# Mixer with seven-tap attention in fp32: h's own ready times in the planner, the u_parts chain cut in two, a fifth tap tile, a fourth val tile

## The chip, the cores and the metric

The kernel runs on one core of one Trainium2 chip. The metric is the time of one execution in microseconds. Before the change three runs took 2129.74, 2135.10 and 2135.57 us, median 2135.1 us.

## The reference

An array x of 8 x 4096 x 192 goes through a seven-tap weighted sum with softmax weights, and the result through an MLP over the tokens and an MLP over the channels:

```python
w = np.exp(weight_gen - max); w = w / (w.sum(-1) + 1e-9)        # 7 taps, 8 heads
x = einsum('bshk,bskhg->bshg', w, windows of 7 rows of x)       # 8 x 4096 x 192
h  = np.maximum(x.transpose(0, 2, 1) @ w_tok1, 0) @ w_tok2      # 4096 -> 256 -> 4096
u  = x + h.transpose(0, 2, 1)
h2 = np.maximum(u @ w_ch1, 0) @ w_ch2                           # 192 -> 1536 -> 192
out = u + h2
```

The weights of the MLPs come as 64-bit floats. Products that must be exact to fp32 are made from a high part and a low part of each operand.

## The kernel before

The 32768 rows are cut into 64 chunks of 512 rows (`NG`), eight to a batch. A prologue makes the tap sums and the first token product of the first batch. Then follow 64 **stages**, one for each chunk g, and the text calls the stage of chunk g "stage g". A stage has the following work.

- **Channel 1** (`channel1`, line 565): six pairs p of PSUM tiles `ph`, 18 matmuls each, from `u_hi` and `u_lo` of chunk g and the resident weights.
- **take_h** (line 577): ScalarE makes the high part of the ReLU (line 579), VectorE the low part (line 580). The tile `h` has four buffers and `ps_w`, from which `ph`, `up` and `th` come, has three. So the fourth `ph` of a stage cannot start until the first `h` has been read by VectorE.
- **Channel 2** (`channel2`, line 584): six times ten matmuls into `acc`; three of them show as x30. The fifth and sixth `h` are taken after its first and second.
- **Token 2** of chunk g+1 (`token2`, line 512; tile `up`): ScalarE copies `xb` into PSUM (line 518), ten matmuls (line 524), ScalarE and VectorE then make `uf` (lines 531 to 536), and `u_parts` (line 538) makes `u_hi` and `u_lo` from it, eight ScalarE copies and two VectorE subtractions, for channel 1 of the next stage. It is one chain: the three copies of lines 550 to 552 stand behind the subtractions of lines 548 and 549.
- **Token 1** of a chunk some eight stages ahead (`token1`, line 475; tile `th`). For the first two batches it is an fp32 product (line 507), after that a product of parts (lines 490 and 492). Its sum over the batch is carried in `h1s`. The last of a batch is followed by `make_h1`, on which token 2 of the next batch rests.
- **Attention** (`attention`, line 204) of two chunks at a time: softmax on `wg`, fourteen products (line 211) and six additions (line 225) on VectorE; the first product goes to `xa`, the other taps to `pr` tiles (four buffers), and GpSimd adds each pair sum to `xa` by DMA (line 229).
- **Store** (`store`, line 638): two transposes on VectorE, twelve ScalarE copies into `out_tile` (line 655), two DMAs.
- **Conversions** in the first stages only: `convert` (line 146) turns 64-bit weights into fp32, three ScalarE and three VectorE operations in a `val` tile, and `split` makes high and low parts. `w2s` is converted in three parts, the last of them in stage 0 (`convert_channel("c2", 2)`, lines 453 to 455).

What runs in which order is set by a planner that runs while the program is built. It keeps estimated clocks `at` of the engines; work waits in chains; `pump` issues from the chains whatever fits before the next matmul group, ScalarE by priority and VectorE by earliest start. The result is one fixed instruction list for each engine, which each engine follows in order.

## Time and profile before

| what | value |
|---|---|
| profiled execution | 2131.6 us |
| its span, first to last instruction | 2129.8 us |
| three runs | 2129.74, 2135.10, 2135.57 us |
| TensorE busy | 2085.4 us, 98% of the span |
| VectorE busy | 1538.5 us, 72% |
| ScalarE busy | 1440.3 us, 68% |
| mean granted TensorE clock | 0.996 |

The times of stages are read from the rows of the TensorE timeline: a stage runs from the first `ph` matmul of its channel 1 to that of the next stage. In a row the number in brackets is the idle time ahead of its first instruction and what ended it.

### The profile page before, as it was taken

Reading aid. Unit: us, or ns where it says so; the run is one execution under the profiler, and the core shown is the slowest. Engines: PE = TensorE matmul, PEld = TensorE weight load, DVE = VectorE, ACT = ScalarE, POOL = GpSimd, SP = SyncE. Lnnn points to the kernel's source line nnn. Section 1 sums busy time; section 2 is a strip of 40 time slices with the busy share of each in tenths; the row PEclk is TensorE's granted clock in tenths of the full one; section 3 lists DMA queues with packets and bytes.
Section 4 is the critical chain, followed back from the end, with each engine's and each line's share of the span. In section 5 each row is a group of like instructions: output and inputs, shape, how many; then the busy total and the mean of one; then the engine's idle time right before and its main releaser. Section 6 shows DMA issues by size and latency. Waiting matters only on the chain.

```text
span 2129.8 us, 32140 instructions
## 1 busy us (share of the span) xinstructions
PE 2085.4 (98%) x12766; PEld 1691.5 (79%) x12766; DVE 1538.5 (72%) x1760; ACT 1440.3 (68%) x2226; POOL 158.2 (7%) x194
## 2 busy tenths in 40 slices
PE   7989899999999999999999999999999999999998
PEld 5767788787878888888888888888888888888887
DVE  8978988788887777777777877777787765343433
ACT  5568666667766766676676677667666766766665
POOL 0001111000100010000000010000100000000000
PEclk9999999999999999999999999999999999999999
DMA  8666757878687667566766756676665655321221
GB/s 279 225 213 171 207 147 210 253 200 230 185 234 202 189 172 190 150 182 181 196 189 173 200 156 174 171 202 193 173 194 149 181 163 148 89 66 45 64 63 23
DMA packets 166198, 363.82 MB, mean 171 GB/s; under 512 B 16552, under 2 KB 105896, under 8 KB 150688
## 3 DMA queue, kind: packets, MB, share of 16 engines
q1 hardware_dynamic: 139808, 285.74, 42.8%
q0 software_dynamic: 25344, 74.46, 17.8%
q8 instruction: 100, 1.64, 0.3%
q10 hardware_dynamic: 896, 1.57, 0.2%
q14 instruction: 50, 0.41, 0.1%
HBM read 225.13 MB, written 70.52 MB: 139 GB/s over the span
## 4 chain that ended last, share of the span: by engine, by line
PE 82%; DVE 10%; ACT 4%; DMA 3%; issue 2%; POOL 0%; SPq 0%; ACTq 0%; DVEq 0%; POOLq 0%
PE acc L591 36%; PE ph L573 33%; PE up L524 7%; PE th L490 3%; DVE h L580 2%; DVE pr L211 2%; PE th L492 1%; DVE prk L327 1%; DMA raw<-in_moe_w_tok_dram 1%; PE th L507 1%; DMA xt<-in_x_dram 1%; DMA xa<-pr 1%; DVE val L160 1%; DVE val L159 1%; DVE pr L225 1%
## 5 line engine op out<-in xcount | busy, mean ns | idle before, releaser
L591 PE MATMUL acc<-h,w2s 128*128 128x512 f32 x3800 | 884.5, 390 | 2.5 <-DVE w2s L454 2.5
L591 PEld LDWEIGHTS acc<-h,w2s 128*128 128x128 f32 x3800 | 709.2, 188 | 148.9 <-DVE w2s L454 2.9
L579 ACT ACTIVATE h<-ph 128x1024 fp32r<-128x1024 f32 x384 | 394.4, 1027 | 396.2 <-PE ph L573 340.1
L580 DVE SCALAR_TENSOR_TENSOR h<-ph,h 128x1024 fp32r<-128x1024 f32 x384 | 467.1, 1217 | 121.3 <-ACT h L579 120.8
L573 PE MATMUL ph<-u_hi,w_hi 64*128 64x512 f32 x2304 | 343.5, 396 | 13.8 <-ACT u_hi L550 5.8
L573 PE MATMUL ph<-u_hi,w_lo 64*128 64x512 f32 x2304 | 332.9, 389 | 0.0
L573 PE MATMUL ph<-u_lo,w_hi 64*128 64x512 f32 x2304 | 332.4, 388 | 0.0
L211 DVE TENSOR_TENSOR pr<-xt,wg 128x768 f32<-128x768 f32 x336 | 314.0, 949 | 8.9 <-DMA xa<-pr 8.1
L573 PEld LDWEIGHTS ph<-u_hi,w_hi 64*128 64x128 f32 x2304 | 216.8, 185 | 82.8 <-issue 21.5
L573 PEld LDWEIGHTS ph<-u_hi,w_lo 64*128 64x128 f32 x2304 | 221.9, 185 | 47.3
L573 PEld LDWEIGHTS ph<-u_lo,w_hi 64*128 64x128 f32 x2304 | 221.8, 185 | 47.4 <-ACT u_lo L554 0.6
L229 POOL DMA_DIRECT2D xa<-pr x168 | 144.6, 861 | 1439.0 <-DVE pr L225 1236.9
L536 DVE TENSOR_TENSOR uf<-up,uf 64x512 f32<-64x512 f32 x63 | 43.0, 682 | 243.2 <-ACT uf L532 243.2
L655 ACT COPY out_tile<-oa 32x256 f32<-32x256 f32 x504 | 203.5, 404 | 7.8
L524 PE MATMUL up<-w,h 128*128 128x512 f32 x630 | 161.7, 402 | 5.9 <-ACT up L518 5.9
L225 DVE TENSOR_TENSOR pr<-pr 128x768 f32<-128x768 f32 x168 | 160.3, 954 | 3.7
L524 PEld LDWEIGHTS up<-w,h 128*128 128x128 f32 x630 | 113.8, 188 | 48.8 <-ACT up L518 16.2
L518 ACT COPY up<-xb 128x1024 f32<-128x1024 f32 x63 | 64.0, 1016 | 84.6 <-DVE h L580 81.5
L490 PE MATMUL th<-xh,w 128*128 128x384 f32 x384 | 112.5, 358 | 1.1 <-ACT th L483 1.1
L655 ACT COPY out_tile<-oc 32x256 f32<-32x256 f32 x252 | 101.6, 403 | 11.0 <-DVE oc L648 6.8
L269 DVE TENSOR_TENSOR xh<-xa,xh 128x768 fp32r<-128x768 f32 x48 | 45.9, 955 | 73.3 <-ACT xh L266 73.3
L492 PE MATMUL th<-xh,w 128*128 128x192 f32 x384 | 96.2, 250 | 0.0
(86 smaller groups left out, 1717.8 us busy)
## 6 DMA issues: line engine op xcount, KB each, us to landing
w<-s SPq DMA_DIRECT2D x96, 1024.0 KB, 5.3
xa<-pr POOLq DMA_DIRECT2D x168, 384.0 KB, 4.9
xt<-in_x_dram SPq DMA_DIRECT2D x56, 960.0 KB, 9.8
out_dram<-out_tile SPq DMA_DIRECT2D x128, 192.0 KB, 3.2
xs<-t SPq DMA_DIRECT2D x58, 384.0 KB, 4.6
xb<-xs SPq DMA_DIRECT2D x348, 64.0 KB, 5.0
raw<-in_moe_w_tok_dram SPq DMA_DIRECT2D x16, 1024.0 KB, 6.0
s<-w POOLq DMA_DIRECT2D x8, 1024.0 KB, 5.3
```

The lines of the kernel that those rows point to most:

```text
L211: nc.vector.tensor_mul(t.rearrange("p t (h g) -> p (t h) g", h=H).rearrange("p (o n) g -> p o n g", o=1), x_k, w)
L225: nc.vector.tensor_add(sums[m], sums[m], prt.pop(m))
L229: nc.gpsimd.dma_start(xat[m].rearrange("p t d -> p (t d)"), sums[m].rearrange("p t d -> p (t d)"), accum_op=ALU.add)
L490: nc.tensor.matmul(th[:, r, 0:2 * D], w[:, c, 0, rs], xh[:, c, :], start=i + c == 0, stop=False, skip_group_check=True)
L492: nc.tensor.matmul(th[:, r, 0:D], w[:, c, 1, rs], xh[:, c, 0:D], start=False, stop=c == CT - 1, skip_group_check=True)
L518: nc.scalar.copy(up.rearrange("p k (n b c) -> p (k n) c b", c=CT, b=Q), xb.rearrange("p k (n c b) -> p (k n) c b", c=CT, b=Q))
L524: nc.tensor.matmul(up[:, n, :], h1[:, k, d], w[:, l, k * N:(k + 1) * N], start=k == 0 and j == 0 and not seeded, stop=k == KR - 1 and j == ...
L573: nc.tensor.matmul(ph[:, j, :], w[rows, k, p * P:(p + 1) * P], u[rows, k], start=n == 0, stop=n == len(steps) - 1)
L579: nc.scalar.activation(h[:, :, 0, :], ph, AF.Relu)
L580: nc.vector.scalar_tensor_tensor(h[:, :, 1, :], ph, 0.0, h[:, :, 0, :].bitcast(F32), op0=ALU.max, op1=ALU.subtract)
L591: nc.tensor.matmul(acc[:, n, :], w2s[:, f, d], h[:, j, l, :], start=False, stop=f == NF - 1 and i == len(steps) - 1, skip_group_check=True)
L655: nc.scalar.copy(dst, src[to:to + Q].rearrange("p (n e d) -> p n e d", n=2, d=Q)[:, n])
```

## The change

- `u_parts` becomes two chains. The first holds `u_hi[:, 0]`, `u_hi[c, 2]`, the subtractions and the three `u_lo` copies, the second the three other `u_hi` copies.
- `PR` goes from 4 to 5.
- `val` gets four buffers outside the prologue pool and two inside (before three and three); `ident` moves into the prologue's pool. The planner waits for a free `val`, and weights of token 1 are fetched two chunks ahead instead of one.
- The planner keeps a ready time for each `h` (`h_at[p]`) and not one for the last. `SLACK_M` is 1000 (400), `LATER` 4000 (5000). An fp32 token 1 no longer waits for the token 1 of the chunk ahead of it.
- A token 1 that is not ready at the usual places may run ahead of the last group of channel 2. The wait for the last part of `w2s` stands ahead of the group that reads it, one group later than before.

```diff
-    PR = 4
+    PR = 5
...
-        pool = pro if pro is not None and n % 6 >= 3 else p1
-        return pool.tile([P, NV], F32, tag="val", name="val", bufs=3)
+        pool = pro if pro is not None and n % 6 >= 4 else p1
+        return pool.tile([P, NV], F32, tag="val", name="val", bufs=2 if pool is pro else 4)
...
+        yield "w", 0, lambda: free["val"]
         v = val_tile()[:, 0:n]
...
-        yield "gate", 0, lambda: state["token1"] >= m - 1
+        if m // NCH >= F1:
+            yield "gate", 0, lambda: state["token1"] >= m - 1
...
+        def first():
+            yield from begin()
+            yield "u", 620, lambda: act(hi[:, 0], ua)
+            yield "u", 620, lambda: act(hi[c, 2], uc[c])
+            yield "n", 0, lambda: taken.update(at=at["act"] + HOP)
+            yield "v", 610, lambda: dve(lo[:, 0], ua, hi[:, 0].bitcast(F32))
+            yield "v", 610, lambda: dve(lo[c, 2], uc[c], hi[c, 2].bitcast(F32))
+            yield "u", 620, lambda: act(lo[c, 1], f[e, 0])
+            yield "u", 620, lambda: act(lo[e, 1], f[c, 0])
+            yield "u", 620, lambda: act(lo[e, 2], f[c, 2])
+            yield "n", 0, last
+
+        def second():
+            yield from begin()
+            yield "gate", 0, lambda: "at" in taken
+            yield "u", 620, lambda: act(hi[c, 1], ua[e])
+            yield "u", 620, lambda: act(hi[e, 1], ua[c])
+            yield "u", 620, lambda: act(hi[e, 2], uc[c])
+            yield "n", 0, last
+        return first(), second()
...
-    LATER = 5000
+    LATER = 4000
...
-    SLACK_M = 400
+    SLACK_M = 1000
...
-        while state["w1"] < min(m + 1 + (m >= F1 * NCH - 3), NG - 1):
+        while state["w1"] < min(m + 2, NG - 1):
...
-        chains.insert(3, Chain(u_parts(m), t, ("u", m)))
+        chains[3:3] = [Chain(items, t, ("u", m)) for items in u_parts(m)]
...
-                if p == 0:
-                    h_at = w_at[-1]
+                h_at[p] = w_at[-1]
...
-                if g == 0:
-                    need(lambda: ("c2", 2) in done, (convert_channel, "c2", 2))
...
+            if g == 0 and p == 2 * NP // 3:
+                need(lambda: ("c2", 2) in done, (convert_channel, "c2", 2))
+            if p == NP - 1:
+                run_picked(picked)
             channel2(g, p)
-            on("pe", C2, free["acc"] if p == 0 else 0.0, h_at)
+            on("pe", C2, free["acc"] if p == 0 else 0.0, h_at[p])
...
+            if p == NP // 2 and token1_ready(C2) and ready[0][0] <= g + NCH:
+                picked = [(do_token1, begin_token1())]
```

The lists of the engines differ in nearly every stage. TensorE's differs in stages 2 to 7 alone, and there in where the eight fp32 token 1 products stand. Three places follow.

**End of stage 0, ScalarE.** Rows `val` of 768 elements belong to the last part of `w2s`, `up` is the copy ahead of token 2 of chunk 1, `h` the sixth of the stage. Before:

```order
L166 CAST w_867<-val 128x1024
L155 ACTIVATE val<-raw 128x768
L156 ACTIVATE val<-val,below 128x768
L518 COPY up<-xb_79 128x8x4x32
L579 ACTIVATE h<-ph 128x2x512
L157 ACTIVATE val<-val 128x768
L155 ACTIVATE val<-raw 128x1024
L181 ACTIVATE wg<-wg 128x448
L531 COPY uf<-up 64x512
L532 COPY uf<-up 128x512
L453 CAST w2s<-val 128x4x192
```

Now:

```order
L165 CAST w_869<-val 128x1024
L520 COPY up<-xb_74 128x8x4x32
L597 ACTIVATE h<-ph 128x2x512
L154 ACTIVATE val<-raw 128x768
L155 ACTIVATE val<-val,below 128x768
L180 ACTIVATE wg<-wg 128x448
L533 COPY uf<-up 64x512
L534 COPY uf<-up 128x512
L156 ACTIVATE val<-val 128x768
L454 CAST w2s<-val 128x4x192
L561 CAST u_hi<-uf 128x512
L562 CAST u_hi<-uf 64x512
```

The two first steps of the conversion now stand behind `up` and the sixth `h`, and its third behind the copies of `uf`.

**Start of stage 3, VectorE.** Rows `oa` and `oc` are the store of stage 2; the last row is the first `h` of stage 3. Before:

```order
L159 SCALAR_TENSOR_TENSOR val<-raw,val 128x1024
L211 TENSOR_TENSOR xa<-xt,wg 128x768
L160 SCALAR_TENSOR_TENSOR val<-raw,val 128x1024
L211 TENSOR_TENSOR xa<-xt,wg 128x768
L645 STREAM_TRANSPOSE oa<-acc 128x512
L646 STREAM_TRANSPOSE oc<-acc 128x512
L648 TENSOR_TENSOR oc<-oc 64x512
L161 SCALAR_TENSOR_TENSOR val<-raw,val 128x1024
L211 TENSOR_TENSOR pr<-xt,wg 128x768
L580 SCALAR_TENSOR_TENSOR h<-ph,h 128x2x512
```

Now:

```order
L291 STREAM_TRANSPOSE t<-xa 128x768
L181 TENSOR_REDUCE mx<-wg 128x64
L158 SCALAR_TENSOR_TENSOR val<-raw,val 128x1024
L663 STREAM_TRANSPOSE oa<-acc 128x512
L664 STREAM_TRANSPOSE oc<-acc 128x512
L666 TENSOR_TENSOR oc<-oc 64x512
L159 SCALAR_TENSOR_TENSOR val<-raw,val 128x1024
L598 SCALAR_TENSOR_TENSOR h<-ph,h 128x2x512
```

The two products into `xa` and the product into `pr` have gone behind the four `h` of the stage.

**Stages 7 and 8, TensorE and ScalarE.** TensorE from the end of channel 1 of stage 7 on; `th` is token 1, `acc` channel 2, `up` token 2 of chunk 8. Before:

```order
L507 MATMUL th<-xa,val 128x192 x8
L591 MATMUL acc<-h,w2s 128x512 x30
L507 MATMUL th<-xa,val 128x192 x8
L591 MATMUL acc<-h,w2s 128x512 x30
L507 MATMUL th<-xa,val 128x192 x8
L524 MATMUL up<-w_2708,h_3145 128x512 x10
```

Now:

```order
L509 MATMUL th<-xa,val 128x192 x8
L609 MATMUL acc<-h,w2s 128x512 x30
L509 MATMUL th<-xa,val 128x192 x8
L609 MATMUL acc<-h,w2s 128x512 x30
L526 MATMUL up<-w_2694,h_3090 128x512 x10
```

The last token 1 of the batch now has a half of channel 2 between itself and token 2. ScalarE in stage 8, from the last `u_hi` of chunk 8 to the first `h`. Before:

```order
L552 CAST u_hi<-uf 64x512
L553 CAST u_lo<-u_lo 64x512
L554 CAST u_lo<-u_lo 64x512
L555 CAST u_lo<-u_lo 64x512
L655 COPY out_tile<-oa 32x8x32 x4
L166 CAST w_3151<-val 128x4x256
L579 ACTIVATE h<-ph 128x2x512 x3
```

Now:

```order
L576 CAST u_hi<-uf 64x512
L566 CAST u_lo<-u_lo 64x512
L567 CAST u_lo<-u_lo 64x512
L568 CAST u_lo<-u_lo 64x512
L673 COPY out_tile<-oc 32x8x32 x2
L673 COPY out_tile<-oa 32x8x32 x4
L673 COPY out_tile<-oc 32x8x32 x2
L673 COPY out_tile<-oa 32x8x32 x4
L165 CAST w_3096<-val 128x4x256
L597 ACTIVATE h<-ph 128x2x512 x3
```

All twelve copies of the store of stage 7 now stand between `u_lo` and the first `h`; before, eight of them came earlier.

More of the change, by code (lines that the diff above doesn't have):

```diff
@@ L56, in mixer_kernel @@
     pro = None
-    ident = const.tile([P, P], F32, name="ident")
-    make_identity(nc, ident)
     below = const.tile([P, 1], F32, name="below")
@@ L411, in last @@
             state["vals"] -= 1
+            free["val"] = at["dve"] + HOP
             w2t[i] = t
@@ L458, in last @@
             state["vals"] -= 1
+            free["val"] = at["dve"] + HOP
             done.add((which, n))
@@ L543, in u_parts, with begin @@
         f, act, dve = lo.bitcast(F32), nc.scalar.copy, nc.vector.tensor_sub
-        yield "gate", 0, lambda: state["channel1"] >= m
-        yield "w", 0, lambda: free["parts"]
-        yield "u", 620, lambda: act(hi[:, 0], ua)
-        yield "u", 620, lambda: act(hi[c, 2], uc[c])
-        yield "v", 610, lambda: dve(lo[:, 0], ua, hi[:, 0].bitcast(F32))
-        yield "v", 610, lambda: dve(lo[c, 2], uc[c], hi[c, 2].bitcast(F32))
-        yield "u", 620, lambda: act(hi[c, 1], ua[e])
-        yield "u", 620, lambda: act(hi[e, 1], ua[c])
-        yield "u", 620, lambda: act(hi[e, 2], uc[c])
-        yield "u", 620, lambda: act(lo[c, 1], f[e, 0])
-        yield "u", 620, lambda: act(lo[e, 1], f[c, 0])
-        yield "u", 620, lambda: act(lo[e, 2], f[c, 2])
-        def last():
-            ut[m] = hi, lo
-            free["u"] = at["act"] + HOP
-        yield "n", 0, last
+        left = [0, 1]
+        taken = {}
+        def begin():
+            yield "gate", 0, lambda: state["channel1"] >= m
+            yield "w", 0, lambda: free["parts"]
+        def last():
+            left.pop()
+            if not left:
+                ut[m] = hi, lo
+                free["u"] = at["act"] + HOP
+        def first():
[17 more added lines that the diff above has]
+        return first(), second()
     ht, acc_t = {}, {}
@@ L696, in mixer_kernel @@
     w_at, h1_at, h1s_at = deque([0.0] * 3), {0: 0.0}, [0.0]
-    free = {"acc": 0.0, "u": 0.0, "t": 0.0, "parts": 0.0, "xh": 0.0}
+    free = {"acc": 0.0, "u": 0.0, "val": 0.0, "t": 0.0, "parts": 0.0, "xh": 0.0}
     pr_free = deque([0.0] * PR)
@@ L794, in mixer_kernel @@
              "summed": NCH - 1, "turned": FT - 1, "parts": NCH - 1, "kept": FT - 1, "stored": -1, "out": -1,
-             "done": NCH - 1, "w1": NCH, "channel1": 0, "rest": 0}
+             "done": NCH - 1, "w1": NCH + 1, "channel1": 0, "rest": 0}
     def raw_free(tag):
@@ L851, in mixer_kernel @@
             tc.tile_pool(name="ps_pro", bufs=1, space=bass.MemoryType.PSUM) as ps_pro:
+        ident = pro.tile([P, P], F32, name="ident")
+        make_identity(nc, ident)
         warm = pro.tile([P, 1], F32, name="warm")
@@ L863, in start @@
             items = iter(items)
-            for _ in range(4):
+            for _ in range(5):
                 next(items)[2]()
@@ L939, in mixer_kernel @@
             nc.tensor.matmul(w[:, j, :], w1_hi[:, 0, 0:P], w1_hi[:, 0, 0:512], start=True, stop=True)
-    run(u_parts(0))
+    run(*u_parts(0))
     free["u"] = 0.0
@@ L947, in mixer_kernel @@
     add_chain(load_w1(NCH))
+    add_chain(load_w1(NCH + 1))
     state["token2"] = 0
@@ L1012, in mixer_kernel @@
     for g in range(NG):
-        phs, kept = {}, {}
+        phs, kept, h_at = {}, {}, {}
         soon = ((convert_w2, 1),) if g == 0 else ()
@@ L1062, in mixer_kernel @@
                 take_h(g, p + HB, phs[p + HB])
-                h_at = on("dve", LOW, on("act", TOP, at["pe"]))
+                h_at[p + HB] = on("dve", LOW, on("act", TOP, at["pe"]))
                 if kept[p] in w_at:
-                    w_at[w_at.index(kept[p])] = h_at
+                    w_at[w_at.index(kept[p])] = h_at[p + HB]
                 if last:
                     picked += list(it)
-                    h_at = 0.0
+            if p == NP // 2 and token1_ready(C2) and ready[0][0] <= g + NCH:
+                picked = [(do_token1, begin_token1())]
         pump(at["pe"] + SLACK_M)
```

## The prediction

> **What bounds the kernel now.** I read the page's busy times and slices first, then the chain that ended last, in order of time, then TensorE's waits, and last the timelines of the three engines around each wait.

> ```profile
> span 2129.8 us, 32140 instructions
> PE 2085.4 (98%) x12766; PEld 1691.5 (79%) x12766; DVE 1538.5 (72%) x1760; ACT 1440.3 (68%) x2226; POOL 158.2 (7%) x194
> PE   7989899999999999999999999999999999999998
> DVE  8978988788887777777777877777787765343433
> PE 82%; DVE 10%; ACT 4%; DMA 3%; issue 2%; POOL 0%; SPq 0%; ACTq 0%; DVEq 0%; POOLq 0%
> ```

> TensorE is the bound, and what it idles it idles in the first slices, where VectorE is nearly as full as TensorE. How long a stage is without waits comes from the chain:

> ```profile
> 319.76 2.60 PE th L507 x16
> ...
> 1000.65 12.49 PE ph L573 x108
> ...
> 1031.54 12.49 PE ph L573 x108
> ...
> 1924.78 12.49 PE ph L573 x108
> ...
> 1953.38 12.49 PE ph L573 x108
> ```

> Channel 1 takes 12.49 us, a stage without token 1 28.60 (1924.78 to 1953.38), with the later token 1 30.89 (1000.65 to 1031.54); an fp32 token 1 adds 2.60, so 31.20. Now the starts of the stages, and the waits that speak for themselves:

> ```profile
> 123.45 0.50 PE L573 MATMUL ph<-u_hi,w_hi 64*128 64x512 f32 x2
> ...
> 154.47 4.85 PE L591 MATMUL acc<-h,w2s 128*128 128x512 f32 x20 [2.46 <-DVE w2s L454]
> ...
> 192.20 0.50 PE L573 MATMUL ph<-u_hi,w_hi 64*128 64x512 f32 x2
> 194.69 1.66 PE L573 MATMUL ph<-u_hi,w_hi 64*128 64x512 f32 x4 [1.99 <-ACT u_hi L550]
> ...
> 227.28 0.97 PE L573 MATMUL ph<-u_hi,w_hi 64*128 64x512 f32 x6
> ...
> 236.84 0.97 PE L573 MATMUL ph<-u_hi,w_hi 64*128 64x512 f32 x6 [3.12 <-DVE h L580]
> ...
> 255.06 4.55 PE L507 MATMUL th<-xa,val 128*128 128x192 f32 x16 [1.81 <-ACT th L483]
> ...
> 266.36 0.97 PE L573 MATMUL ph<-u_hi,w_hi 64*128 64x512 f32 x6
> ```

> ```profile
> 396.88 2.56 PE L524 MATMUL up<-w,h 128*128 128x512 f32 x10 [2.35 <-ACT up L518]
> 401.41 0.49 PE L573 MATMUL ph<-u_hi,w_hi 64*128 64x512 f32 x2 [1.97 <-ACT u_hi L546]
> 402.77 1.95 PE L573 MATMUL ph<-u_hi,w_hi 64*128 64x512 f32 x4 [0.86 <-ACT u_hi L550]
> ...
> 418.34 2.58 PE L524 MATMUL up<-w,h 128*128 128x512 f32 x10
> ...
> 436.74 0.97 PE L573 MATMUL ph<-u_hi,w_hi 64*128 64x512 f32 x6
> ...
> 629.98 0.97 PE L573 MATMUL ph<-u_hi,w_hi 64*128 64x512 f32 x6
> ```

> These rows give the excess over stages without waits, waits and slow matmuls together. Stages 0 and 1: 192.20 - 123.45 - 57.20 = 11.55 us. Stage 2: 35.08 - 31.20 = 3.88. Stage 3: 39.08 - 31.20 = 7.88. Stages 4 to 8 (six fp32 token 1, one later one): 170.38 - 160.89 = 9.49. Stages 9 to 14: 193.24 - 6 x 30.89 = 7.90. In all **40.7 us**; this is the most that any order of the same matmuls can gain behind the prologue. From 629.98 on stages run at their length.

> ```profile
> PE ph L573 <- ACT u_hi L550: 5.8, 4, 2.0
> PE ph L573 <- DVE h L580: 5.5, 4, 3.1
> ```

> Two lines of TensorE's waits: `u_hi` is late four times and `h` four times. The change works on both.

> **The change part by part.** The prologue keeps its list on TensorE, and `ident` is needed first at 11.8 us; I cost its move at nothing, hidden behind the first tap products. No matmul is added or removed.

> *Stages 0 to 2.* The last part of `w2s` comes later:

> ```profile
> 147.98 0.84 ACT L157 ACTIVATE val<-val 128x768 f32<-128x768 f32 x1
> ...
> 153.12 0.83 ACT L453 CAST w2s<-val 128x768 fp32r<-128x768 f32 x1 [1.61 <-DVE val L161]
> ```

> The third step stood at 147.98, now it stands behind both copies of `uf`, which end near 151.3 whatever stands ahead. It ends at 152.2, three VectorE steps of 0.95 end at 155.1, the cast at 155.9, the first subtraction (0.42) at 156.4. TensorE then waits until 156.4 and not 154.47: **2.0 us lost**. In return all `u_hi` are ready at 159, ahead of channel 1. But four `val` steps of 1.1 us now stand ahead of the `u_lo` copies, which end near 165.2, and channel 1 of stage 1 uses them 1.6 us after its start: the first group ends some 1.4 us later than before. Stage 1 comes out 0 to 2 us later. In stage 2 the 1.99 us for `u_hi` and some 1.7 us of slow matmuls behind it go. What is late next is `h`: VectorE is full from the sixth `h` of stage 1 to the first of stage 2 (nine steps, the store, two products and an addition ahead of it, some 14 us), and I work out 1.7 us for the fourth `ph`. Together I take -0.5, with bounds of -5 (the `u_hi` waits of stages 1 and 2, 3.4, and 1.7 of slow matmuls go, nothing comes) and +4 (2.0 for `w2s`, 2 for stage 1).

> [...] The trace does not follow the gap's length: after 3.12 us at 236.84 six matmuls take 0.97 as without a wait, while after 1.81 us at 255.06 sixteen take 4.55. [...]

> *Stage 3.* Ahead of its first `h` VectorE had two `xa` products, a `val` step and a `pr` product:

> ```profile
> 233.56 1.22 DVE L161 SCALAR_TENSOR_TENSOR val<-raw,val 128x1024 uint32<-128x1024 uint32 x1
> 234.71 0.95 DVE L211 TENSOR_TENSOR pr<-xt,wg 128x768 f32<-128x768 f32 x1
> 235.57 1.22 DVE L580 SCALAR_TENSOR_TENSOR h<-ph,h 128x1024 fp32r<-128x1024 f32 x1
> ...
> 253.49 1.14 ACT L155 ACTIVATE val<-raw 128x1024 f32<-128x1024 f32 x1 [1.29 <-DVE w L167]
> 254.54 0.47 ACT L483 COPY th<-h1s 128x384 f32<-128x384 f32 x1
> ```

> From the fifth `h` of stage 2 to the first of stage 3 the new list has one `val` step, two `xa`, one `pr`, and two small softmax steps less and one reduction more: 1.2 + 1.9 + 0.95 + 0.75 - 0.6 = 4.2 us less. The `h` came 3.12 us late, so that wait goes, and the 0.57 behind it for `up` nearly. The 1.81 for `th` came from a `val` step ahead of it that waited 1.29 us for a `val` buffer; with four buffers and another order it stands elsewhere, and with it go 1.8 of slow matmuls. 3.12 + 0.4 + 1.81 + 1.8 = 7.1, and I take the rest of the excess too, **-7.5** (bounds -7.9 and -4, if one of the two waits stays in half).

> *Stages 4 to 6* have almost no excess. New is that in stage 5 both `xa` products stand ahead of the store, some 8 us after the x tiles could be loaded:

> ```profile
> 473.04 0.96 DVE L211 TENSOR_TENSOR xa<-xt,wg 128x768 f32<-128x768 f32 x1 [1.57 <-DMA xt<-in_x_dram]
> ...
> 501.47 0.96 DVE L211 TENSOR_TENSOR pr<-xt,wg 128x768 f32<-128x768 f32 x1 [2.41 <-DMA xa<-pr]
> ```

> The first row shows such a product waiting 1.57 us for its tile. I take +0.7 (0 to +2).

> *Stages 7 and 8.* With channel 2 between the last token 1 and token 2, the 2.35 us ahead of 396.88 go. What is late next is the first `h` of stage 8:

> ```profile
> 405.71 1.65 ACT L655 COPY out_tile<-oa 32x256 f32<-32x256 f32 x4
> ...
> 408.33 1.02 ACT L579 ACTIVATE h<-ph 128x1024 fp32r<-128x1024 f32 x1
> ```

> Four copies of 0.41 stood between `u_lo` and it, now twelve: it starts 3.3 us later, 14.8 us after token 2's start. Its VectorE half, 1.3 later and 1.2 long, ends at 17.2; the fourth `ph` started at 15.1 (418.34 less three groups of 2.08, less 396.88). So 2.1 us come back, and the sum is -0.25. Bounds: -2.35 and +2.

> *Stages 9 to 14.* The waits for `h` (0.75, 0.33 and 1.30 of the 5.5 above) came from the two waits of VectorE just shown. In the new list the `xa` products of stage 10 stand behind the third `h`, six microseconds later, and the fifth `pr` tile lets a product start that had to wait for the addition by DMA two sums back. Products there now come behind the landing. Of 7.90 I leave 1.4, **-6.5** (bounds -7.9 and -3).

> *The other 49 stages*: the sum of VectorE's steps from the store to the fourth `h` is 10.1 us where it was 11.0 in the fuller stages, so nothing new is late. 0.

> Sum: -0.5 - 7.5 + 0.7 - 0.25 - 6.5 = -14.05, say -14. The profiled execution took 2131.6; **2117.5 us**. That execution stands 3.5 us below the median of the three runs, so against the median the same step would read 2121.

> **The rivals.** (1) *The waits go without a substitute.* The `h` of stages 2 and 8 are on time too, and the clock stays up in stage 8, where channel 1 took 15.6 in place of 12.49. For it: TensorE's order needs nothing else. Against: the twelve copies. Stages 0 to 2 -4, stage 3 -7.9, 7 and 8 -5, the later ones -7.9: -25, 2107.

> (2) *VectorE is the bound of the early stages.* Its slices read 9, 8, 8, 7 and 8 there; waits move from one stage to the next and only the products that really left early stages count, and the `xt` wait of stage 5 is full. Stage 3 -4, the later ones -3, stages 0 to 2 +2: -5, 2126.6.

> (3) *Slower: `up` is late in every second stage.*

> ```profile
> 1011.92 1.02 ACT L518 COPY up<-xb 128x1024 f32<-128x1024 f32 x1 [1.73 <-DVE h L580]
> ```

> It ends at 1012.94, token 2 starts at 1013.14: 0.2 us of room. Some 20 stages are built like this one. If the fourth `h` comes one product (0.95) later than now, by larger slack in the planner or a product that waits for its `pr` tile, each loses 0.75, 15 us, which eats the gain; with -5 in the early stages the time is 2141. It decides from 0.2 us on. Against it: the list ahead of that `h` is shorter.

> (4) *The change leaves time as it is*, each wait replaced by another of its size: 2131.6.

> **How the numbers follow.** Forecast 0.55, (1) 0.17, (2) 0.17, (3) 0.05, (4) 0.06. The forecast's own range by half of its bounds is 2111 to 2125. For 8 in 10 the range reaches to (1) and to (2) with the 3.5 us to the median: 2107 to 2129. A difference of 0.3%, 6.4 us, is about what a measurement of this kernel can tell from none. Faster by more than that: the forecast, (1) and half of (2), 0.81. Within: the other half, and (4), 0.14. Slower: (3), 0.05.

> **What would show it.** Right: the start of stage 4 near 258 (now 266.36) with no wait for `h` in stage 3; a `w2s` wait of 4 to 5 us in stage 0; no wait for `u_hi` in stages 1 and 2; token 2 of chunk 8 without a wait, then a wait for `h` of about 2 us in stage 8; stages 9 to 14 near 30.9 to 31.3 each; later stages at 30.89. Wrong: `h` waits in stages 1, 2 and 5 of more than 2 us each, or any wait that recurs after stage 16.

## The result, and the profile after

| | before | after |
|---|---|---|
| profiled execution | 2131.6 us | 2116.5 us |
| its span | 2129.8 us | 2114.7 us |
| median of four runs | 2133.6 us (2129.74 to 2135.57) | 2116.6 us (2114.93 to 2118.70) |
| ratio after to before | | 0.9924, 95% interval 0.9910 to 0.9939 |

The change makes the kernel 0.76% faster. The profiled execution came out at 2116.5 us where 2117.5 was forecast. But a sum can be right with wrong terms, so first the same rows of the TensorE timeline as before, now of the changed kernel: starts of stages, and the waits that are left (start, duration, instruction, in brackets the idle time ahead and what ended it).

```profile
124.07 0.50 PE L591 MATMUL ph<-u_hi,w_hi 64*128 64x512 f32 x2
...
156.25 6.47 PE L609 MATMUL acc<-h,w2s 128*128 128x512 f32 x20 [4.05 <-DVE w2s L455]
162.65 0.97 PE L591 MATMUL ph<-u_hi,w_hi 64*128 64x512 f32 x6
...
171.30 0.97 PE L591 MATMUL ph<-u_hi,w_hi 64*128 64x512 f32 x6 [1.79 <-DVE h L598]
...
193.99 0.97 PE L591 MATMUL ph<-u_hi,w_hi 64*128 64x512 f32 x6
...
226.29 0.97 PE L591 MATMUL ph<-u_hi,w_hi 64*128 64x512 f32 x6
...
257.50 0.97 PE L591 MATMUL ph<-u_hi,w_hi 64*128 64x512 f32 x6
...
354.05 0.97 PE L591 MATMUL ph<-u_hi,w_hi 64*128 64x512 f32 x6
...
390.19 0.50 PE L591 MATMUL ph<-u_hi,w_hi 64*128 64x512 f32 x2 [2.25 <-ACT u_hi L561]
...
402.97 1.65 PE L591 MATMUL ph<-u_hi,w_hi 64*128 64x512 f32 x6 [2.71 <-DVE h L598]
...
429.33 0.97 PE L591 MATMUL ph<-u_hi,w_hi 64*128 64x512 f32 x6
...
614.92 0.97 PE L591 MATMUL ph<-u_hi,w_hi 64*128 64x512 f32 x6
```

One more row of before, the start of stage 7:

```profile
360.32 0.97 PE L573 MATMUL ph<-u_hi,w_hi 64*128 64x512 f32 x6
```

Differences of these starts, beside those of the rows shown of before, give the terms. Where the number of fp32 token 1 products differs, it is the excess over stages without waits that is compared (28.60, plus 2.60 for each fp32 token 1, plus 2.29 for a later one): stages 4 to 6 hold four of them now and three before, stages 7 and 8 two and three.

| piece | before | after | measured | forecast |
|---|---|---|---|---|
| up to stage 0 | 123.45 | 124.07 | +0.62 | 0 |
| stages 0 to 2 | 103.83 | 102.22 | -1.61 | -0.5 |
| stage 3 | 39.08 | 31.21 | -7.87 | -7.5 |
| stages 4 to 6, excess | 93.96 - 93.60 = 0.36 | 96.55 - 96.20 = 0.35 | 0.0 | +0.7 |
| stages 7 and 8, excess | 76.42 - 67.29 = 9.13 | 75.28 - 64.69 = 10.59 | +1.46 | -0.25 |
| stages 9 to 14 | 193.24 | 185.59 | -7.65 | -6.5 |
| from stage 15 to the end | 1499.82 | 1499.78 | 0.0 | 0 |
| sum | | | -15.1 | -14 |

The gain stands where it was expected, in stage 3 and in stages 9 to 14. Most of what is left of the excess stands in stage 0 (38.58 us, ten over its length) and in stages 7 and 8; stage 1 has 2.74 and stage 2 1.10. The wait for `h` in stage 8 is the one forecast, but nothing was gained there in all. The 0.62 us up to stage 0 are within the scatter: in the traces of the runs below stage 0 starts between 123.15 (e9) and 124.80 (e7), and in the two that edit the kernel before at 123.34 (e11) and 124.06 (e12).

### The profile page after: what moved, and what is told of

Same layout as the page of the kernel before. It is cut to its first block, busy times and chain, and to the rows that moved or that the text cites. A ratio compares the mean times of both kernels' runs of the same rounds, so it can differ in the third digit from the quotient of the medians.

```text
span 2114.7 us, 32148 instructions
## 1 busy us (share of the span) xinstructions
PE 2080.1 (98%) x12766; PEld 1691.5 (80%) x12766; DVE 1541.0 (73%) x1760; ACT 1444.5 (68%) x2226; POOL 157.7 (7%) x194
## 3 DMA queue, kind: packets, MB, share of 16 engines
q10 hardware_dynamic: 896, 1.57, 0.2%
## 4 chain that ended last, share of the span: by engine, by line
PE 94%; DVE 3%; ACT 2%; DMA 1%; issue 0%; POOL 0%; SPq 0%; ACTq 0%; DVEq 0%; POOLq 0%
PE acc L609 40%; PE ph L591 36%; PE up L526 7%; PE th L492 4%; PE tapsum L338 2%; PE th L494 2%; PE th L509 1%; DVE h L598 0%; DMA xt<-in_x_dram 0%; PE acc L626 0%; DVE prk L327 0%; PE turn L348 0%; DVE val L159 0%; DMA raw<-in_moe_w_tok_dram 0%; DVE val L160 0%
## 5 line engine op out<-in xcount | busy, mean ns | idle before, releaser
L591 PE MATMUL ph<-u_hi,w_hi 64*128 64x512 f32 x2304 | 338.2, 395 | 9.7 <-DVE h L598 4.5
L591 PE MATMUL ph<-u_hi,w_lo 64*128 64x512 f32 x2304 | 329.5, 389 | 0.0
L591 PE MATMUL ph<-u_lo,w_hi 64*128 64x512 f32 x2304 | 329.2, 388 | 0.0
L591 PEld LDWEIGHTS ph<-u_hi,w_hi 64*128 64x128 f32 x2304 | 214.0, 185 | 76.6 <-issue 20.1
L591 PEld LDWEIGHTS ph<-u_lo,w_hi 64*128 64x128 f32 x2304 | 219.8, 185 | 46.8 <-ACT u_lo L568 0.3
L591 PEld LDWEIGHTS ph<-u_hi,w_lo 64*128 64x128 f32 x2304 | 219.2, 185 | 47.0
```

The lines of the kernel that those rows point to most:

```text
L591: nc.tensor.matmul(ph[:, j, :], w[rows, k, p * P:(p + 1) * P], u[rows, k], start=n == 0, stop=n == len(steps) - 1)
```

## The experiments

Most change one thing; e6, e8 and e9 put several edits together. All but e8 and e9 are single runs, and single times scatter by some 2 us either way, as the four runs of the changed kernel do, so they are read by their stages.

Even a stage with the same lists does not always take the same time. Stage 0 takes 38.58 us in the changed kernel, 37.74 in e1, 39.40 in e5 and 37.79 in e6; stage 8 takes 39.14, in e1 37.53 and in e7 40.15. The difference goes with where TensorE's granted clock is halved (last section): in stage 0 it stands at 0.50 for 6.8 us in the changed kernel (126.5 to 129.9 and 157.2 to 160.6), for 10.4 us in e5 (127.3 to 130.8 and 154.6 to 161.5) and for 3.5 us in e6 (156.2 to 159.7). What stays is the start of the fourth `ph` of stage 8, 12.78 us behind the first in the changed kernel, e1 and e7, so that is what a change of stage 8 is read from.

### Is it the fifth tile or the place in the list? (e1)

```diff
-            t = p1.tile([P, CT, D], F32, tag="pr", name="pr", bufs=PR)
+            t = p1.tile([P, CT, D], F32, tag="pr", name="pr", bufs=PR - 1)
```

> The changed kernel with its lists on all engines as they are, but only four pr tiles in memory (the planner still counts five). My theory for stages 9 to 14 had two parts: the xa products stand behind the third h, and a fifth pr tile lets a product start before the addition by DMA has landed. By it some of the waits come back: stages 9 to 14 take 1 to 3 us more than the 185.6 they take now, stage 3 stays at 31.2, time 2117.5 to 2120. Rival A: the place in the list alone did it: every stage within 0.1 us, 2116.5. Rival B: the fifth tile is all of it: stages 9 to 14 near 193, 2124.

Measured 2115.2 us. First its TensorE timeline at the starts of stages 9 and 15, then VectorE's waits (engine, line and what it waited for: sum, times, longest) of before and of this run.

```profile
427.73 0.50 PE L591 MATMUL ph<-u_hi,w_hi 64*128 64x512 f32 x2
...
613.62 0.73 PE L591 MATMUL ph<-u_hi,w_hi 64*128 64x512 f32 x4
```

```profile
DVE pr L211 <- DMA xa<-pr: 8.1, 4, 3.2
```

```profile
DVE pr L210 <- DMA xa<-pr: 9.1, 11, 2.7
```

Stages 9 to 14 take 185.89 us with four tiles and 185.59 with five, and stage 3 takes 31.21 with both: Rival A holds there within 0.3. The second row shows why my half of the theory was plausible and still wrong. With four tiles VectorE does wait for the addition by DMA, eleven times, 9.1 us in all; with five the waits view of the changed kernel has no such row. But in the new list these waits lie behind the `h`, and TensorE does not see them, beyond 0.24 us at one `up` in stage 11 and 0.78 at one `h` in stage 7, which takes 1.12 us more.

### Is it the planner's time for each h? (e2, e12)

e2 takes the edit out of the changed kernel:

```diff
-                h_at[p] = w_at[-1]
+                if p == 0:
+                    h_at = w_at[-1]
...
-            on("pe", C2, free["acc"] if p == 0 else 0.0, h_at[p])
+            on("pe", C2, free["acc"] if p == 0 else 0.0, h_at)
```

> The changed kernel, with the planner's single ready time of h as before (all other edits stay). Theory: h's own times are what moves the xa products behind the h of stage 3 and of stages 9 to 14; without them the waits for h come back, 3 us in stage 3 and 2 to 4 in stages 9 to 14: 2121 to 2125. Rival: the other edits (slack, tiles, two chains) made the good list: 2115 to 2118, stage 3 at 31.2 plus 2.6 for each fp32 token 1 beyond the first.

e12 puts the same edit, the other way round, into the kernel before, and nothing else.

> The kernel before with one edit: the planner keeps a ready time for each h. Theory: this edit makes the lists of stages 3 and 9 to 14 good by itself: the waits for h go there (stages 9 to 14 within 1 us of 30.9 each, stage 3 without its 3.1), while the u_hi waits of stages 1 and 2 stay; token 1 of chunk 16 is no longer in stage 8 and two token 1 stand in stage 15, which costs some 9 to 11 us in stages 15 and 16: 2124 to 2131. Rival: it needs the larger slack and the other edits; stages 9 to 14 keep 4 us or more of their 7.9: 2133 to 2142.

e2 took 2171.7 us, far worse than either theory. Its waits of TensorE:

```profile
PE th L492 <- ACT th L485: 27.2, 36, 2.0
PE ph L591 <- DVE h L598: 13.8, 8, 4.6
```

`h` is late eight times (twice in the changed kernel), and `th` is late 36 times, by 1.17 us in every second steady stage. Stage 3 has 2.92 us of excess again (`h` late by 1.70), and stages 9 to 14 take 195.26. Without the edit the other edits make a list that is worse than the one before them.

e12 took 2152.4 us. Its TensorE timeline at the starts of stages 3, 4, 7, 8, 9 and 15, with two token 1 in stage 7 between:

```profile
222.30 0.50 PE L573 MATMUL ph<-u_hi,w_hi 64*128 64x512 f32 x2
...
253.68 0.50 PE L573 MATMUL ph<-u_hi,w_hi 64*128 64x512 f32 x2
...
348.00 0.50 PE L573 MATMUL ph<-u_hi,w_hi 64*128 64x512 f32 x2
...
389.55 4.51 PE L507 MATMUL th<-xa,val 128*128 128x192 f32 x16 [8.09 <-ACT th L483]
402.75 4.73 PE L507 MATMUL th<-xa,val 128*128 128x192 f32 x16 [8.69 <-ACT th L483]
...
415.68 0.50 PE L573 MATMUL ph<-u_hi,w_hi 64*128 64x512 f32 x2 [1.97 <-ACT u_hi L546]
...
448.88 0.50 PE L573 MATMUL ph<-u_hi,w_hi 64*128 64x512 f32 x2
...
634.43 0.50 PE L573 MATMUL ph<-u_hi,w_hi 64*128 64x512 f32 x2
```

Stage 3 takes 31.38 us, and stages 9 to 14 take 185.55, as in the changed kernel. So this edit alone brings the gain of both places, and the theory of this run holds there. It does not hold for stages 1 and 2, where the waits for `u_hi` were to stay: with `u_parts` in one chain, 0.28 us of them is left, and the wait for `w2s` is 4.05 us as in the changed kernel. Nor does it hold for the sum: the eight fp32 token 1 now stand so late that four of them fall into stage 7, which takes 67.68 us where 28.60 + 4 x 2.60 = 39.00 are work. The third waited 8.09 us and the fourth 8.69 for ScalarE, which itself waited for weights ahead of the fourth copy:

```profile
401.26 1.04 ACT L166 CAST w<-val 128x1024 fp32r<-128x1024 f32 x1 [6.64 <-DMA val<-s]
```

The changed kernel has two of the eight in stage 7. Its other edits (a third place for a late token 1, weights two chunks ahead, the larger slack) are what can move them forward; which of them does was not taken apart.

### What u_parts in two chains and PR 5 do to the list (e3, e10, e11)

e3 has `u_parts` as it was before, e10 has `PR = 4` in planner and memory, e11 is the kernel before with `PR = 5`:

```diff
-        chains[3:3] = [Chain(items, t, ("u", m)) for items in u_parts(m)]
+        chains.insert(3, Chain(u_parts(m), t, ("u", m)))
```

> The changed kernel with u_parts as one chain again. Theory: u_hi is late again at the start of stages 1 and 2 (1.4 and 2.0 us, with 1.7 of slow matmuls behind one of them): 2119 to 2122. Rival: u_hi was late before because steps of the w2s and w2 conversions stood ahead of it on ScalarE, and these have moved by other edits; then stages 1 and 2 stay at 31.3 and 32.3 and the time at 2116 to 2118.

> The changed kernel with PR 4, in the planner and in memory (all other edits stay). In memory alone a fourth tile less cost nothing; here the lists change too: token 1 of chunk 16 is no longer in stage 8 and two token 1 stand in stage 15. Theory: the planner's fifth tile is what lets it put products behind the h; stages 9 to 14 have waits for h again, 2 to 6 us, and the end of the batch in stages 15 and 16 costs 9 to 11 us as in the run with one chain: 2126 to 2133. Rival: the lists of stages 9 to 14 stay as good as now, only stages 15 and 16 cost: 2122 to 2126.

> The kernel before with PR 5 alone, in the planner and in memory. Theory: the fifth tile lets the planner put products elsewhere, but without h's own ready times and the larger slack the waits for h in stages 3 and 9 to 14 stay in part: 2124 to 2131. Rival A: PR alone brings the gain of stages 9 to 14 (7.7 us): 2122 to 2125. Rival B: it makes a worse list: 2134 to 2145.

Measured: 2131.2, 2136.2 and 2152.6 us. In e3 `u_hi` is late again at one of the two places, by 1.51 us in stage 2; in stage 1 it is `h`, by 3.02 us. Stages 0 to 2 cost 106.78 us, 4.6 more. What was not in the expectation is the larger part, the end of the next batch (TensorE's timeline, starts of stages 15, 16 and 17):

```profile
617.83 0.50 PE L575 MATMUL ph<-u_hi,w_hi 64*128 64x512 f32 x2
...
653.00 0.50 PE L575 MATMUL ph<-u_hi,w_hi 64*128 64x512 f32 x2 [1.98 <-ACT u_hi L548]
...
691.01 0.50 PE L575 MATMUL ph<-u_hi,w_hi 64*128 64x512 f32 x2
```

Stages 15 and 16 take 73.18 us where they took 61.76. The list has lost one token 1 in stage 8, so two stand in stage 15, token 2 comes last in the stage, and channel 1 of stage 16 waits for its `u_hi`, as in stage 8. e10 and e12 lose the same one and pay there too. e10's stages 9 to 14 are as good as in the changed kernel (622.32 - 437.00 = 185.32), which is its rival for these stages; what it loses besides is in stage 7 (51.54 us, one `th` late by 7.62). e11 is a worse list, as in its Rival B: `h` is late seven times and `up` once by 5.45. All three times lie above every range that was expected.

So neither the tile nor the chains act only where they were put in; through the planner they move other work. In e3, e10 and e12 that is a token 1, which slips from stage 8 to the end of the batch and costs stages 15 and 16 some 9 to 11 us beyond its own 2.29. In e11 the token 1 stand where they stood before, and the loss is in stages 3, 6 and 7, which are 2.9, 6.0 and 5.2 us longer.

### Late h in stage 8: the copies or VectorE? (e5, e6)

The forecast put the late `h` on twelve `out_tile` copies. In the changed kernel ScalarE and VectorE ahead of it, timeline of each:

```profile
394.48 0.81 ACT L673 COPY out_tile<-oc 32x256 f32<-32x256 f32 x2
...
397.81 1.65 ACT L673 COPY out_tile<-oa 32x256 f32<-32x256 f32 x4
399.48 1.05 ACT L165 CAST w<-val 128x1024 fp32r<-128x1024 f32 x1
400.43 2.84 ACT L597 ACTIVATE h<-ph 128x1024 fp32r<-128x1024 f32 x3
```

```profile
391.49 1.81 DVE L210 TENSOR_TENSOR pr<-xt,wg 128x768 f32<-128x768 f32 x2
...
398.80 0.96 DVE L224 TENSOR_TENSOR pr<-pr 128x768 f32<-128x768 f32 x1
400.56 1.23 DVE L166 TENSOR_TENSOR w<-val,w 128x1024 fp32r<-128x1024 f32 x1 [0.80 <-ACT w L165]
401.70 3.48 DVE L598 SCALAR_TENSOR_TENSOR h<-ph,h 128x1024 fp32r<-128x1024 f32 x3
```

VectorE is busy with products until 399.76, so both engines are late by nearly the same time. e5 moves the copies alone. ScalarE's list in stage 8:

```diff
 CAST u_lo<-u_lo 64x512
-COPY out_tile x12
 CAST w<-val 128x4x256
 ACTIVATE h<-ph 128x2x512 x3
+COPY out_tile x2
 COPY acc<-uf 128x1024
 ACTIVATE h<-ph 128x2x512
 COPY up<-xb 128x8x4x32
+COPY out_tile x4
 ACTIVATE wg<-wg 128x448
 COPY uf<-up 64x512
 COPY uf<-up 128x512
+COPY out_tile x6
```

> The changed kernel; only the twelve out_tile copies of stage 7 stand behind the third h of stage 8 on ScalarE (two of them), behind up (four) and behind uf (six). All other lists as they are. The step of the prediction: the twelve copies make the first h late. By it the wait of 2.71 us for h goes and the second slow stretch (1.7) with it: stage 8 takes 34.7 us (39.1 now), 2112. Rival: VectorE has six products and three additions ahead of that h, which end at 399.8, and the w step behind them; then h comes only 0.7 us earlier, stage 8 takes 38.4, 2116.

e6 moves six products and three additions of VectorE as well, behind the second, third and fourth `h`.

> As the run before, and the products and additions that VectorE had ahead of the first h of stage 8 stand one behind the second h, one behind the third, the rest behind the fourth. If ScalarE and VectorE are both late there, only this run removes the wait: stage 8 34.7 us, 2112, where the run before gave about 38.4. If the copies alone were it, both runs give 34.7. Rival: the moved work makes up, the fifth h or stage 9 late: stage 8 or 9 longer by 1 to 3 us, 2113 to 2115.

TensorE in e5, then in e6: the start of stage 8, the wait in it, the start of stage 9.

```profile
391.30 0.50 PE L591 MATMUL ph<-u_hi,w_hi 64*128 64x512 f32 x2 [2.25 <-ACT u_hi L561]
...
403.19 0.50 PE L591 MATMUL ph<-u_hi,w_hi 64*128 64x512 f32 x2 [1.91 <-DVE h L598]
...
429.54 0.50 PE L591 MATMUL ph<-u_hi,w_hi 64*128 64x512 f32 x2
```

```profile
388.87 0.50 PE L606 MATMUL ph<-u_hi,w_hi 64*128 64x512 f32 x2 [2.25 <-ACT u_hi L576]
...
422.41 0.66 PE L507 MATMUL th<-xh,w 128*128 128x384 f32 x1 [7.72 <-DVE xh L284]
...
433.28 0.50 PE L606 MATMUL ph<-u_hi,w_hi 64*128 64x512 f32 x2
```

e5 took 2117.6 us: the fourth `ph` starts 11.89 us behind the first (403.19 - 391.30), 0.89 earlier than in the changed kernel, stage 8 takes 0.90 less (38.24), and stage 9 gives 0.93 back. That is the rival, 0.7 us. In e6 the wait for `h` is gone, so the copies and the products together made `h` late. The products alone were not moved; in the changed kernel VectorE already waits 0.80 us for ScalarE's `w` ahead of its first `h` (the row of 400.56), so with the copies in place little could come of it, but that is argued and not run. In e6 token 1 of chunk 16, halfway through channel 2 of the same stage, now waits 7.72 us for `xh`, because the sum of chunk 16 is made of the products that were moved (e9 below bears this out). Stage 8 takes 44.41 us and the run 2120.6. That is neither expectation: the products are not in the way by mistake, they are due.

### The clock behind the waits (e4)

e4 adds matmuls that write a tile nobody reads, 14 in the wait for `w2s` and 9 ahead of channel 1 of stage 8:

```diff
+    def fill(n):
+        w = ps_w.tile([P, 2, 512], F32, tag="w", name="w")
+        for j in range(n):
+            nc.tensor.matmul(w[:, j % 2, :], w1_hi[:, 0, 0:P], w1_hi[:, 0, 0:512], start=True, stop=True)
```

> The changed kernel with its lists as they are and two fillers on TensorE that write a PSUM tile nobody reads: 14 matmuls in the wait for w2s in stage 0 (3.2 of 4.05 us) and 9 between token 2 of chunk 8 and channel 1 of stage 8 (2.0 of 2.25 us). Theory: the matmuls behind these two waits are slow because the clock is halved for 3.4 us after a stretch that was idle for some 1.5 us or more; with the gaps filled the clock stays up, stage 0 takes 1.6 us less (37.0), stage 8 1.2 to 3.4 less (36 to 38), 2112 to 2114. Rival: the matmuls behind the waits are slow for another reason (their operands come one by one): all stages as they are, 2116.5; or the fillers get in the way of the next ph tile: stage 8 longer by 0.5 to 2.

TensorE by windows (start and end, length, busy time and matmuls, granted clock, then DMA), of the changed kernel and of e4:

```profile
157.20:160.60 3.40, 3.40 (x10) 0.50 1.02 363
...
392.70:396.10 3.40, 3.39 (x16) 0.51 0.55 103
...
402.90:406.30 3.40, 3.33 (x16) 0.51 1.01 262
```

```profile
157.20:160.60 3.40, 3.40 (x18) 1.00 1.06 347
...
392.70:396.10 3.40, 3.40 (x34) 1.00 0.78 146
...
399.20:402.50 3.30, 1.95 (x10) 0.50 1.07 222
```

e4 took 2115.0 us. With the gaps filled the clock stays up behind both (1.00 in the windows from 157.20 and from 392.70, where the changed kernel has 0.50 and 0.51), so the slow matmuls come from the idle time and not from late operands. With the wait of 4.05 us unfilled the matmuls behind it meet half the clock in the changed kernel (from 157.2 us), e5 (from 154.6, inside the wait), e6 (from 156.2), e10 (from 157.5) and e12 (from 157.4), so this is not chance. The 3.4 us of the theory are what the changed kernel shows, 3.42 to 3.44 for each of its stretches ahead of 420 us; that some 1.5 us of idle time is enough was an estimate, and no run shows a limit (the last section has 3.12 us with no half clock behind it). Stage 0 takes 36.18 us, 2.4 less than in the changed kernel. About 1.6 of that is the filler's, as expected: e6 takes 37.79, and has no slow stretch near 126.5 us (1.00 in all its windows from 100 to 156.2). The other 0.8 is what e6 too has less than the changed kernel; that e4 also lacks that stretch is an estimate from these times. In stage 8 nothing is won (40.07): its fourth `ph` starts 12.8 us behind the first in both runs (402.97 - 390.19, 400.55 - 387.75), when ScalarE and VectorE let it; the faster matmuls ahead only wait longer, 3.86 us, and the clock is halved from inside that wait on (0.50 in the windows from 399.2 to 405.9). So the half clock ahead of this wait costs nothing: the changed kernel has it from 392.7 to 396.2 us, e4 does not, and the fourth `ph` starts 12.78 and 12.80 us behind the first. Behind the wait it costs: with half clock from 402.96 to 406.40 the changed kernel takes 26.36 us from the fourth `ph` to the start of stage 9. e1 takes 24.75 there, and its stage 8 37.53 in place of 39.14; that it has no half clock there is an estimate from these times, as 3.4 us at half clock cost 1.7 us.

### The conversion earlier, and all together (e7, e8, e9)

e7 moves the steps of the last `w2s` conversion. ScalarE's list in stage 0; on VectorE its three `val` steps move from behind `uf` to behind the sixth `h`:

```diff
 ACTIVATE val<-val 128x1024
+ACTIVATE val<-raw 128x768
+ACTIVATE val<-val,below 128x768
+ACTIVATE val<-val 128x768
 ACTIVATE h<-ph 128x2x512
 CAST w<-val 128x1024
 COPY up<-xb 128x8x4x32
 ACTIVATE h<-ph 128x2x512
-ACTIVATE val<-raw 128x768
-ACTIVATE val<-val,below 128x768
 ACTIVATE wg<-wg 128x448
 COPY uf<-up 64x512
 COPY uf<-up 128x512
-ACTIVATE val<-val 128x768
 CAST w2s<-val 128x4x192
```

> The changed kernel; the three ScalarE steps of the last w2s conversion stand ahead of the fifth h of stage 0 (where ScalarE is idle for 3.4 us) and its three VectorE steps behind the sixth. All other lists as they are. Theory: the wait of 4.05 us comes only from the conversion's place; it falls to below 1 us and the slow matmuls behind it (1.6) go: stage 0 33.5 to 34.2 us (38.6 now), stage 1 31.3, 2111 to 2112. Rival: what is late next takes it back, VectorE's val steps ahead of the first h of stage 1 or u_hi itself: stage 1 up to 34, 2113 to 2115.

> The changed kernel with the edits of the two runs before together and a filler of nine matmuls between token 2 of chunk 8 and channel 1 of stage 8. If the losses left in stages 0 and 8 are the late conversion, the work ahead of the first h, and the halved clock behind the waits, their sizes add: 4.7 (stage 0), 4.4 (stage 8) and 1.7 (the first slow stretch of stage 8): 2116.5 - 10.8 = 2105.7, between 2104 and 2109. If a wait takes the place of one of them, 2110 to 2114.

> As the run with all three edits, but of VectorE's nine product steps ahead of the first h of stage 8 the first three (two products, an addition) stay there, where VectorE was idle for 4.0 us, and the other six stand between and behind the first four h, so that the sum of chunk 16 is done some 3 us earlier than in that run. Theory: the 8.0 us that token 1 of chunk 16 waited there came from its sum, whose additions by DMA follow these products; stage 0 at 33 to 34, stage 8 at 32 to 34, 2104 to 2107. Rival: the sum still lands behind the middle of channel 2: a wait of 1 to 4 us for xh, stage 8 34 to 37, 2107 to 2111.

e7 took 2113.3 us; its TensorE timeline at the wait and at the start of stage 1 (stage 0 starts at 124.80):

```profile
153.94 0.50 PE L650 MATMUL acc<-h,w2s 128*128 128x512 f32 x1 [0.74 <-DVE w2s L168]
...
158.70 0.50 PE L632 MATMUL ph<-u_hi,w_hi 64*128 64x512 f32 x2
```

The wait falls from 4.05 to 0.74, stage 0 to 33.90 (4.7 less, as expected), and stage 1 stays at 31.34. The time lies above the 2111 to 2112 expected, not for the rival's reason: stage 0 starts 0.73 us later than in the changed kernel, and stage 8, whose lists are the same, takes 40.15 us. e8, with e6's and e7's edits and the filler, was to be 2104 to 2109 and is 2115.1 (five runs, 2113.01 to 2115.66): what e6 lost at token 1 of chunk 16 it loses again, 8.04 us. e9 leaves three product steps where VectorE was idle and spreads the other six, VectorE's list in stage 8:

```diff
 TENSOR_TENSOR pr<-xt,wg x2
 TENSOR_TENSOR pr<-pr
-TENSOR_TENSOR pr<-xt,wg x2
-TENSOR_TENSOR pr<-pr
-TENSOR_TENSOR pr<-xt,wg x2
-TENSOR_TENSOR pr<-pr
 TENSOR_TENSOR w<-val,w
-SCALAR_TENSOR_TENSOR h<-ph,h x3
-TENSOR_TENSOR pr<-xt,wg x2
 SCALAR_TENSOR_TENSOR h<-ph,h
+TENSOR_TENSOR pr<-xt,wg
+SCALAR_TENSOR_TENSOR h<-ph,h
+TENSOR_TENSOR pr<-xt,wg
+SCALAR_TENSOR_TENSOR h<-ph,h
+TENSOR_TENSOR pr<-pr
+TENSOR_TENSOR pr<-xt,wg
+SCALAR_TENSOR_TENSOR h<-ph,h
+TENSOR_TENSOR pr<-xt,wg
+TENSOR_TENSOR pr<-pr
+TENSOR_TENSOR pr<-xt,wg x2
 TENSOR_TENSOR pr<-pr
```

Its TensorE timeline at stage 8, at that token 1, and at stage 9:

```profile
384.00 0.50 PE L650 MATMUL ph<-u_hi,w_hi 64*128 64x512 f32 x2
...
410.70 0.41 PE L551 MATMUL th<-xh,w 128*128 128x384 f32 x1 [1.63 <-DVE xh L326]
...
419.94 0.50 PE L650 MATMUL ph<-u_hi,w_hi 64*128 64x512 f32 x2
```

Stage 8 takes 35.94 us (39.14 in the changed kernel), stage 9 pays 1.7, and the median of four runs is 2108.8 us (2108.31 to 2111.61), in the range of its rival. Its ratio to the kernel before is 0.9883 (0.9862 to 0.9905), below the interval of the change, so e9 beats both kernels.

## Why the prediction was right, step by step

**What bounds the kernel** was read rightly: the excess of the first 15 stages could be won, and nothing behind them moved (0.0 of 1499.8 us). Of the sums that set its range, half of the bounds gives 2113 us at the lower end and not 2111, and (2) with 3.5 us gives 2130 and not 2129; nothing hangs on either.

**Stage 3** (-7.5, measured -7.87) went as worked out: no wait for `h`, `up` or `th` is left. The cause is the planner's time for each `h`: with it alone the stage is as short (e12), without it `h` is late again (e2).

**Stages 9 to 14** (-6.5, measured -7.65): the size was right and half of the mechanism fell. "The fifth `pr` tile lets a product start that had to wait" is true on VectorE (9.1 us of waits in e1, none with five tiles) but not on the path: with four tiles the stages are as short. The place of the products behind the `h` is enough, and that came from the `h` times alone.

**Stages 0 to 2** (-0.5, measured -1.61): the wait for `w2s` was put at 156.4 and ended at 156.25; all `u_hi` waits of stages 1 and 2 went, as forecast, though not by the two chains alone: they nearly go in e12, which has one chain, they stay away in e2, which has two chains and one `h` time, and one of the two comes back in e3; `h` is late by 1.79 us, but in stage 1, where I had 1.7 in stage 2. The sum has no slow matmuls behind the wait for `w2s`, and they came: the 20 matmuls took 6.47 us against 4.85 before, 1.6 more, with the clock at 0.50 from 157.2 to 160.6 us. Stage 0 lost 2.78 us (35.80 to 38.58), but with `u_hi` on time stage 1 gained 1.61 and stage 2 2.78, more than I had let them.

**Stages 4 to 6** (+0.7, measured 0.0): the wait for the x tiles did not come. VectorE waited 1.6 us for `xt` at an `xa` product before, and has no such row now.

**Stages 7 and 8** (-0.25, measured +1.46) is the step that failed, by 1.7 us. "So 2.1 us come back": 2.71 came, from the place named and at the time worked out (the fourth `ph` starts 402.97 - 385.51 = 17.46 us behind token 2, where 17.2 was forecast), but the cause was half named. The twelve copies alone cost 0.9 (e5); nine steps on VectorE stood beside them, and they are due for token 1 of chunk 16 (e6). And the sum had no slow matmuls behind the new wait: 3.4 us at half clock (402.96 to 406.40), 1.7 us lost. This is the part that makes the 1.7, and it changes from run to run. From the fourth `ph` to the start of stage 9 the same list takes 24.75 us in e1, 26.36 in the changed kernel and 27.37 in e7, where the first two matmuls behind the wait take 0.80 us (398.75) and the first two of the stage 0.50 (385.97). Stage 8 takes 37.53, 39.14 and 40.15 us; with stage 7 of the changed kernel the term would be -0.15 with e1's, as good as forecast, and in e7 it is +2.18. So the wait was sized rightly, its cause was half named, and the half clock behind it, which the sum put at nothing, is worth 0 to 2.6 us from run to run, an estimate from these three times.

**The rivals.** (1), 2107, asked for no substitute anywhere; stages 0 and 8 have them. (2), VectorE as the bound, fits at most stage 8, where it shares the wait with ScalarE, and the 1.79 us of stage 1. (3) did not come in the changed kernel; e2 shows a relative of it, a `th` late in every second stage, so the danger was real. The errors partly cancelled, -3.3 us in four terms (stages 0 to 6 and 9 to 14) against +1.7 in stages 7 and 8 and +0.6 ahead of stage 0: the sum of the prediction is better than its terms, and that it came within 1 us is in part luck.

## What to carry to other kernels

Where a planner makes the order, undo an edit in the planner and in memory apart: the fifth tile was worth nothing as memory (e1) and 20 us as a number that the planner counts with (e10, one run). A time that the planner keeps too coarsely (one ready time for six `h`) cost more than either tile here, 55 us in e2, and correcting it alone can still lose (e12), because other work that must be done by a due time slips behind. Work ahead of a late operand is not always misplaced: ask who needs it, and by when, before moving it.

## What the runs showed of the hardware

```profile
234.90:238.30 3.40, 1.46 (x12) 1.00 0.00 0
238.30:241.70 3.40, 3.40 (x32) 1.00 0.16 27
252.00:255.40 3.40, 1.59 (x8) 1.00 1.02 201
255.40:258.80 3.40, 3.40 (x13) 0.51 0.68 281
```

A window with 1.46 us of work left the clock up, one with 1.59 was followed by half of it. What tells these two apart stays open.
